# Four half-step curves in place of five whole-step curves for the exp on VectorE

## The chip, the cores and the metric

One core of one Trainium2 chip. Times are device microseconds (us) of one execution. "PE" in a profile is TensorE's matmuls, "PEld" its weight loads, "DVE" VectorE, "ACT" ScalarE, "POOL" GpSimd, "SP" SyncE.

## The reference

```python
x  = A_x                                # 1 x 2048 x 512, bf16
xn = layernorm(x)
q  = (xn @ wq)  as 32 heads of 16       # one key and one value head for all of them
k, v = xn @ wk, xn @ wv                 # 2048 x 16 each
p  = softmax(q k^T * 16**-0.5)          # 32 x 2048 x 2048 values of exp
s  = (p v) @ wo
g  = silu(silu(xn @ w1) @ w2)           # w1 512 x 1792, w2 1792 x 512
return x + s * g
```

The 32 x 2048 x 2048 = 134 million exps are what costs. In tiles of 128 keys x 512 queries they are 2048 "slots", in 32 groups of 64 (a group is four heads, one block of 512 queries and 16 blocks of 128 keys).

## The kernel before

Each slot's scores come from TensorE into a PSUM bank, go through exp, and the result is multiplied with v on TensorE. Two engines share the exps:

- ScalarE takes two or three slots in one exp instruction (128 x 1024 or 128 x 1536).
- VectorE is given no exp instruction. It writes the *bit pattern* of an approximate power of two: score x 128/ln 2 + offset, rounded to an integer and read as bf16. That is exact at powers of two and up to 6% too large between them. So five such curves, shifted by fifths of an octave, are weighted and added: the first is the pattern itself, the others are the pattern plus 25, 51, 77 and 102. The weights sit in five copies of v, so TensorE does the adding, with one product per curve.

```python
SHIFT = (0, 25, 51, 77, 102)
SHIFT_W = (0.2265625, 0.19726562, 0.17480469, 0.14941406, 0.12988281)
SHIFT_BETA = -0.239948630
K = len(SHIFT)
```

The instruction order is not written out by hand. A planner in the kernel, run when the kernel is built, simulates the engines with fixed durations and puts each next instruction where it fits. It is greedy: any small change can shift what it chooses later. It makes scores in turns called phases, each with two or three banks for ScalarE and up to two slots for VectorE. It decides slot by slot who computes an exp:

```python
        def want_d(banks_left=True):
            if st["assigned"] < 8:
                return False
            if any(k not in evac_kt or evac_kt[k].op is None for k in range(NKT)):
                return False
            if dve_backlog() > DVE_LIMIT:
                return False
            return True

...
                        cap = len([b for b in pool_free if pl.ready(PE, (), [("ps", b)]) <= t + 30])
                        bl = dve_backlog()
                        want = 2 if bl < TWO_LIMIT else 1
                        nd = min(cap, 4 - len(banks), len(need), want)
                        if nd < min(want, len(need)) and len(banks) == 3 and bl < LEND_LIMIT:
                            nd, lend = nd + 1, True
                        for i in need[:nd]:
```

So VectorE gets a slot when one of two spare PSUM banks is free (`pool_free`; the MLP's jobs borrow them too), or when a bank is lent from ScalarE's three, and its queue is short. ScalarE takes the other slots of the phase:

```python
                op = pl.place(AC, 0.8333 * NQ * n + T_AF, lambda a: a.activation(
                    pa_sb[:, s, 0:n * NQ], ps[:, b0 * 512:(b0 + n) * 512], ACT.Exp),
                    [("ps", b) for b in u.banks[:n]], [("pA", s)])
```

VectorE's part: one operation out of PSUM per slot (the pattern goes to `db_sb`, and its product is queued at once), and, for each batch of four slots, K - 1 = 4 shifts into `ds_sb`. A shift is one VectorE operation on 128 x 2048, or four GpSimd operations on 128 x 512, whichever engine gets to it first:

```python
                    tot[g, i] += K

                    def placed(pop, b=b, g=g, i=i, kt=kt, bt=bt):
                        if b in POOL_BANKS:
                            pool_free.append(b)
                        pvq[g][i].append((pop, v_lhs(0 + 1, g, kt), db_sb[:, bt.b, i * NQ:(i + 1) * NQ].bitcast(BF16),
                                          [("Db", bt.b, i)] + v_reads(1, kt), ("b", bt)))
                    bt.P[i] = pl.add(Task(DV, T_P, lambda v, b=b, i=i, bb=bt.b: v.tensor_scalar(
                        db_sb[:, bb, i * NQ:(i + 1) * NQ], bank(b), 128.0 * LOG2E, 128.0 * SHIFT_BETA + 16256.0,
                        op0=ALU.mult, op1=ALU.add), [("ps", b)], [("Db", bt.b, i)], 2 if b in POOL_BANKS else 0, on_place=placed))
...
            sh.whole = pl.add(Task(DV, T_SH, lambda v: v.tensor_scalar(
                ds_sb[:, s, :], db_sb[:, bt.b, :], SHIFT[j], None, op0=ALU.add),
                [("Db", bt.b, i) for i in range(4)], ds_keys(s),
                lambda: URGENT if bt.g == st["gO"] and nleft[bt.g] <= CLOSING else 6,
                list(bt.P.values()), on_place=placed_dv, ports=2))
            sh.chunks = []
            for i in range(4):
                tk = Task(PO, T_PC, lambda g, i=i: g.tensor_scalar(
                    ds_sb[:, s, i * NQ:(i + 1) * NQ], db_sb[:, bt.b, i * NQ:(i + 1) * NQ], 1.0, SHIFT[j],
                    op0=ALU.mult, op1=ALU.add),
                    [("Db", bt.b, i)], [("Ds", s, i)], (0 if i else 1, -len(shifts), i), list(bt.P.values()),
                    on_place=lambda pop, i=i: placed_po(pop, i),
                    gate=lambda i=i: (sh.owner is None if i == 0 else sh.owner == PO and sh.chunks[i - 1].op is not None)
                    and beside_psum_read(), ports=2)
...
        def beside_psum_read():
            if not pl.order[DV]:
                return False
            last = pl.order[DV][-1]
            return last.ports == 1 and last.end - max(pl.clk[PO], pl.lock[DV], pl.lock[PO]) >= PC_FIT * T_PC
```

The last function lets GpSimd start, in the plan, only beside a VectorE instruction that reads PSUM.

The softmax here doesn't subtract the row's maximum and nothing guards it: scores larger than these inputs give would overflow.

## Time and profile before

| | before |
|---|---|
| time, median of 3 runs | 750.44 us (750.18 to 750.54) |
| profiled span | 748.0 us |
| ScalarE busy | 727.6 us, 97% |
| TensorE busy | 709.1 us, 95% |
| VectorE busy | 703.7 us, 94% |
| GpSimd busy | 498.1 us, 67% |
| slots on ScalarE / VectorE | 1508 / 540 |
| exp instructions | 701 |

The page of the kernel before: its span, the busy time of each engine (us, share, instructions), and the chain of work that ended last, by engine and by line.

```profile
span 748.0 us, 21011 instructions
...
PE 709.1 (95%) x8809; PEld 200.9 (27%) x8809; DVE 703.7 (94%) x1226; ACT 727.6 (97%) x780; POOL 498.1 (67%) x686
...
ACT 95%; DVE 1%; PE 1%; DMA 1%; POOL 0%; issue 0%; SPq 0%; ACTq 0%; DVEq 0%
ACT pa_sb L1272 91%; ACT t_sb L539 4%; ACT t_sb L562 1%; DMA ds_sb<-in_A_x_dram 1%; DVE stats_sb L373 0%; PE ps L412 0%; POOL v_sb L496 0%; SPq L331 0%; PE ps L428 0%; DVE xn_sb L389 0%; PE ps L1034 0%; PE ps L711 0%; ACTq L277 0%; DVE ob_sb L579 0%; POOL rstd_sb L385 0%
```

Three engines are over 90% busy, so busy shares alone do not say which one sets the time. The chain does: followed back from the end, 95% of the span is ScalarE and 91% one line, the exp of score slots.

The table by stretches of the kernel before: stretch and length, then busy us and (instructions) of each engine, TensorE's granted clock, DMA share, GB/s.

```profile
core 0: us, PE busy (x) PEld busy (x) DVE busy (x) ACT busy (x) POOL busy (x), PEclk, DMA share, GB/s
0.00:25.00 25.00, 21.20 (x215) 10.23 (x219) 21.14 (x63) 14.07 (x16) 14.56 (x33) 0.93 0.90 296
...
300.00:400.00 100.00, 96.62 (x1212) 26.42 (x1204) 93.79 (x158) 100.00 (x107) 68.28 (x91) 1.00 0.01 2
...
700.00:735.00 35.00, 33.98 (x420) 9.13 (x420) 33.28 (x58) 35.00 (x39) 22.61 (x31) 1.00 0.01 2
```

After the start-up ScalarE is busy all of the time; VectorE and TensorE have 3 to 6% left.

Two pieces of the chain in order of time (start, length, what):

```profile
46.80 5.01 ACT pa_sb L1272 x5
...
99.11 4.58 ACT pa_sb L1272 x5
```

The second is five two-slot exps; the first, longer by just one slot, has one three-slot exp among four two-slot ones. So a two-slot exp takes 4.58 / 5 = 0.916 us from start to start and the three-slot one 5.01 - 4 x 0.916 = 1.346 us. The difference, 0.43 us, is the price of a slot on ScalarE; 0.916 - 2 x 0.43 = about 0.06 us is the fixed part of an instruction.

The groups of instructions of the kernel before: line, engine, operation, output<-input, shapes, count | busy us, mean ns of one | idle us of the engine just before, and what ended it.

```profile
L1272 ACT ACTIVATE pa_sb<-ps 128x1024 bf16<-128x1024 f32 x595 | 603.2, 1272 | 1.4 <-PE ps L711 1.3
L954 POOL TENSOR_SCALAR ds_sb<-db_sb 128x512 uint16<-128x512 uint16 x640 | 478.2, 758 | 215.1 <-DVE ds_sb L947 101.1 <-DVE db_sb L887 77.0 <-DVE otr_sb L1055 10.8
L887 DVE TENSOR_SCALAR db_sb<-ps 128x512 uint16<-128x512 f32 x540 | 357.2, 682 | 23.3 <-PE ps L711 21.2
L1034 PE MATMUL ps<-ds_sb,v_sb 128*32 128x512 bf16 x2160 | 286.7, 382 | 0.2
L711 PE MATMUL ps<-qt_sb,kt_sb 32*128 32x512 bf16 x2048 | 275.2, 384 | 28.4 <-ACT pa_sb L1272 14.7 <-DVE kt_sb L468 1.0 <-DVE f_sb L1051 1.0
...
L947 DVE TENSOR_SCALAR ds_sb<-db_sb 128x2048 uint16<-128x2048 uint16 x380 | 249.6, 682 | 1.5
L1272 ACT ACTIVATE pa_sb<-ps 128x1536 bf16<-128x1536 f32 x106 | 177.7, 1676 | 1.4 <-PE ps L711 1.4
L1034 PE MATMUL ps<-db_sb,v_sb 128*32 128x512 bf16 x540 | 145.0, 384 | 1.6 <-DVE f_sb L1051 1.6
```

595 x 2 + 106 x 3 = 1508 slots on ScalarE, and 540 on VectorE: 135 batches with 540 shifts, of which VectorE does 380 and GpSimd 160 (640 chunks / 4). The "mean ns" of an exp, 1272, is longer than its 0.916 us from start to start: successive instructions overlap, so a mean duration is no price. ScalarE's idle time before its exps is 2.8 us in all.

The waits of the kernel before: who waited for whom, us in total, times, longest.

```profile
PEld ps L711 <- ACT pa_sb L1272: 238.8, 514, 1.0
POOL ds_sb L954 <- DVE ds_sb L947: 101.1, 81, 3.5
```

TensorE's weight loads wait for ScalarE 238.8 us (a score bank is free only when exp has read it), ScalarE hardly ever for TensorE. GpSimd waits 101.1 us for VectorE's shifts. The Trainium skill ("SBUF — State Buffer", section "Who interferes with whom") says that VectorE in its two-port modes and GpSimd hold a shared port pair one at a time; this wait, put there by the planner's rule above, is how the plan keeps them apart. On the chip it does so only in part, and the trace agrees with the page: 384 of the 640 chunks meet no VectorE shift (less than 30 ns of it) and take 621 ns on average; the other 256 do and take 963 ns, and over all chunks the duration rises with the time shared (correlation 0.99). Of all 640 the least, median and greatest are 611, 618 and 1122 ns. So the mean of 758 ns is a mixture of the two kinds. (GpSimd's records are rough, so the sizes are too.)

### The profile page before, as it was taken

The numbers are of one execution on the slowest core, as the hardware profiler recorded it, in microseconds if no ns is written. First come the engines' busy times: TensorE is split into PE (matmuls) and PEld (weight loads), VectorE is DVE, ScalarE is ACT, GpSimd is POOL, SyncE is SP. The second block draws the span as 40 slices with busy tenths as digits, with TensorE's granted clock in tenths as the row PEclk, the third lists the DMA queues.
The fourth block names the chain that finished last, engine by engine and source line by source line (L and its number), as shares of the span: only waits on it lengthen the run. The fifth ranks groups of instructions, "written<-read, shape, count | busy, mean of one in ns | idle before, by whom it ended". The sixth has DMA issues, their size and how long they took to land.

```text
span 748.0 us, 21011 instructions
## 1 busy us (share of the span) xinstructions
PE 709.1 (95%) x8809; PEld 200.9 (27%) x8809; DVE 703.7 (94%) x1226; ACT 727.6 (97%) x780; POOL 498.1 (67%) x686
## 2 busy tenths in 40 slices
PE   8899999999999999999999999999999999999996
PEld 4322222222222222222222222222222222222222
DVE  8699999999999999998998999999999999999995
ACT  5899999999999999999999999999999999999994
POOL 5468674567767846766686766677678586676770
PEclk9999999999999999999999999999999999999999
DMA  9300000000000000000000000000000000000000
GB/s 314 95 4 2 2 1 2 2 2 3 2 1 16 11 21 16 1 3 2 2 2 3 15 20 26 2 2 2 1 2 2 16 16 15 16 2 2 2 2 29
DMA packets 11437, 12.65 MB, mean 17 GB/s; under 512 B 1808, under 2 KB 10768, under 8 KB 11344
## 3 DMA queue, kind: packets, MB, share of 16 engines
q1 hardware_dynamic: 10288, 11.28, 4.7%
q8 instruction: 71, 1.16, 0.6%
q10 hardware_dynamic: 1056, 0.03, 0.1%
q14 instruction: 22, 0.18, 0.1%
HBM read 8.95 MB, written 2.10 MB: 15 GB/s over the span
## 4 chain that ended last, share of the span: by engine, by line
ACT 95%; DVE 1%; PE 1%; DMA 1%; POOL 0%; issue 0%; SPq 0%; ACTq 0%; DVEq 0%
ACT pa_sb L1272 91%; ACT t_sb L539 4%; ACT t_sb L562 1%; DMA ds_sb<-in_A_x_dram 1%; DVE stats_sb L373 0%; PE ps L412 0%; POOL v_sb L496 0%; SPq L331 0%; PE ps L428 0%; DVE xn_sb L389 0%; PE ps L1034 0%; PE ps L711 0%; ACTq L277 0%; DVE ob_sb L579 0%; POOL rstd_sb L385 0%
## 5 line engine op out<-in xcount | busy, mean ns | idle before, releaser
L1272 ACT ACTIVATE pa_sb<-ps 128x1024 bf16<-128x1024 f32 (+1 forms) x701 | 715.5, 1333 | 2.8 <-PE ps L711 2.7
L954 POOL TENSOR_SCALAR ds_sb<-db_sb 128x512 uint16<-128x512 uint16 x640 | 478.2, 758 | 215.1 <-DVE ds_sb L947 101.1
L887 DVE TENSOR_SCALAR db_sb<-ps 128x512 uint16<-128x512 f32 x540 | 357.2, 682 | 23.3 <-PE ps L711 21.2
L711 PE MATMUL ps<-qt_sb,kt_sb 32*128 32x512 bf16 x2048 | 275.2, 384 | 28.4 <-ACT pa_sb L1272 14.7
L1034 PE MATMUL ps<-ds_sb,v_sb 128*32 128x512 bf16 x2160 | 286.7, 382 | 0.2
L1034 PE MATMUL ps<-pa_sb,v_sb 128*32 128x512 bf16 x1508 | 267.2, 385 | 1.1 <-ACT pa_sb L1272 0.7
L947 DVE TENSOR_SCALAR ds_sb<-db_sb 128x2048 uint16<-128x2048 uint16 x380 | 249.6, 682 | 1.5
L711 PEld LDWEIGHTS ps<-qt_sb,kt_sb 32*128 32x128 bf16 x2048 | 72.3, 91 | 332.6 <-ACT pa_sb L1272 238.8
L1034 PE MATMUL ps<-db_sb,v_sb 128*32 128x512 bf16 x540 | 145.0, 384 | 1.6 <-DVE f_sb L1051 1.6
L1034 PEld LDWEIGHTS ps<-ds_sb,v_sb 128*32 128x32 bf16 x2160 | 71.8, 95 | 54.7 <-issue 32.4
L412 PE MATMUL ps<-w_sb,u_sb 128*32 128x512 bf16 x896 | 79.0, 385 | 0.0
L412 PE MATMUL ps<-xnT_sb,w_sb 128*32 128x512 bf16 x896 | 76.3, 384 | 0.5 <-DVE u_sb L541 0.3
L1034 PEld LDWEIGHTS ps<-pa_sb,v_sb 128*32 128x32 bf16 x1508 | 64.1, 95 | 46.0 <-issue 31.7
L539 ACT ACTIVATE t_sb<-ps 128x512 bf16<-128x512 f32 x56 | 48.1, 858 | 0.0
L1034 PEld LDWEIGHTS ps<-db_sb,v_sb 128*32 128x32 bf16 x540 | 35.2, 94 | 17.3 <-issue 8.6
L541 DVE SCALAR_TENSOR_TENSOR u_sb<-t_sb,ps 128x512 bf16<-128x512 bf16 x56 | 38.0, 678 | 1.8 <-ACT t_sb L539 1.8
L412 PEld LDWEIGHTS ps<-xnT_sb,w_sb 128*32 128x32 bf16 x896 | 19.5, 94 | 31.7 <-issue 22.7
L412 PEld LDWEIGHTS ps<-w_sb,u_sb 128*32 128x32 bf16 x896 | 19.8, 94 | 30.5 <-issue 27.6
L1051 DVE STREAM_TRANSPOSE f_sb<-ps 128x512 f32<-128x512 f32 x32 | 22.6, 706 | 5.4 <-PE ps L1034 5.4
L412 PE MATMUL ps<-xnT_sb,wq_sb 128*32 128x512 bf16 x256 | 22.0, 384 | 0.2 <-DVE db_sb L887 0.2
L412 PE MATMUL ps<-wo_sb,on_sb 128*32 128x512 bf16 x256 | 20.0, 383 | 0.0
L496 POOL TENSOR_SCALAR v_sb<-v_sb 128x64 bf16<-128x64 f32 x24 | 8.9, 373 | 9.4 <-DVE v_sb L492 6.1
(47 smaller groups left out, 174.1 us busy)
## 6 DMA issues: line engine op xcount, KB each, us to landing
w_sb<-in_B_w_dram SPq DMA_DIRECT2D x2, 1792.0 KB, 13.6
xr_sb<-in_A_x_dram SPq DMA_DIRECT2D x16, 128.0 KB, 2.3
out_dram<-ob_sb SPq DMA_DIRECT2D x16, 128.0 KB, 1.7
ds_sb<-in_A_x_dram SPq DMA_DIRECT2D x3, 512.0 KB, 6.9
ds_sb<-in_A_x_dram SPq DMA_DIRECT2D x4, 128.0 KB, 2.6
wq_sb<-in_A_wq_dram SPq DMA_DIRECT2D x1, 512.0 KB, 5.0
wo_sb<-in_A_wo_dram SPq DMA_DIRECT2D x1, 512.0 KB, 15.3
kt_sb<-kt_sb SPq DMA_DIRECT2D x4, 64.0 KB, 2.3
```

The costliest lines, as they stand in the source:

```text
L412: last = h.matmul(bank(b)[32 * j:32 * (j + 1), 0:n], lhsT=lhs(j), rhs=rhs, start=start, stop=stop, tile_position=(0, 32 * j), skip_group_c ...
L496: v_task[c, j] = pl.add(Task(PO, 150.0, lambda g, j=j: g.tensor_scalar(v_sb[:, j, 4 * c:4 * c + 4, DH:2 * DH], v32_sb[:, 4 * c:4 * c + 4, ...
L539: t1 = Task(AC, 477.0, lambda a: a.activation(t_sb[:, k, :], bank(b), ACT.Tanh, scale=0.5), [("ps", b)], [("t", k)], 0)
L541: t2 = Task(DV, T_P, lambda v: v.scalar_tensor_tensor(out=u_sb[:, ft, :], in0=t_sb[:, k, :], scalar=1.0, in1=bank(b), op0=ALU.add, op1=ALU ...
L562: t1 = Task(AC, 477.0, lambda a: a.activation(t_sb[:, k, :], bank(b), ACT.Tanh, scale=0.25), [("ps", b)], [("t", k)], 0)
L711: return pe.matmul(bank(b), lhsT=kt_sb[32 * i:32 * i + 32, g % 2, kt * P:(kt + 1) * P], rhs=qt_sb[32 * i:32 * i + 32, (g // 2) % NQR, :], ...
L887: bt.P[i] = pl.add(Task(DV, T_P, lambda v, b=b, i=i, bb=bt.b: v.tensor_scalar(db_sb[:, bb, i * NQ:(i + 1) * NQ], bank(b), 128.0 * LOG2E, 1 ...
L947: sh.whole = pl.add(Task(DV, T_SH, lambda v: v.tensor_scalar(ds_sb[:, s, :], db_sb[:, bt.b, :], SHIFT[j], None, op0=ALU.add), [("Db", bt.b ...
L954: tk = Task(PO, T_PC, lambda g, i=i: g.tensor_scalar(ds_sb[:, s, i * NQ:(i + 1) * NQ], db_sb[:, bt.b, i * NQ:(i + 1) * NQ], 1.0, SHIFT[j], ...
L1034: h = pe.matmul(bank(OB)[32 * i:32 * (i + 1), :], lhsT=lhs, rhs=rhs, start=s0, stop=s1, tile_position=(0, 32 * i), skip_group_check=True)
L1051: t1 = pl.add(Task(DV, T_TR, lambda v: v.transpose(f_sb[:, k, :], bank(OB)), [("ps", OB)], [("F", k)], 1, [norm.get(("m", g - 2))]))
L1272: op = pl.place(AC, 0.8333 * NQ * n + T_AF, lambda a: a.activation(pa_sb[:, s, 0:n * NQ], ps[:, b0 * 512:(b0 + n) * 512], ACT.Exp), [("ps" ...
```

## The change

Its intent: four curves with the accuracy of five, and so four products per VectorE slot on TensorE, not five. VectorE keeps the pattern with one more bit of fraction (256 steps per octave). It is no longer a bf16 number, so it is never multiplied itself; each of the four shifts adds its amount and halves, and the rounding of the half goes down in two of the curves and up in the other two. The first product of a slot must now wait for a shift. A last clause lets GpSimd finish shifts at the end of the plan, when no PSUM read is left to work beside.

```diff
-SHIFT = (0, 25, 51, 77, 102)
-SHIFT_W = (0.2265625, 0.19726562, 0.17480469, 0.14941406, 0.12988281)
-SHIFT_BETA = -0.239948630
+SHIFT = (-0.5, 64.5, 127.5, 192.5)
+SHIFT_W = (0.24609375, 0.20703125, 0.173828125, 0.146484375)
+SHIFT_BETA = -0.035
...
-    NDB, NDS = 4, 2 * (K - 1)
+    NDB, NDS = 4, 2 * K
...
-            ... bt.left = g, {}, free[0], {}, 0, 4 + K - 1
+            ... bt.left = g, {}, free[0], {}, 0, K
...
-                        pvq[g][i].append((pop, v_lhs(0 + 1, g, kt), db_sb[...].bitcast(BF16), ...))
...
-                        db_sb[...], bank(b), 128.0 * LOG2E, 128.0 * SHIFT_BETA + 16256.0,
+                        db_sb[...], bank(b), 256.0 * LOG2E, 256.0 * (SHIFT_BETA + 127.0),
...
-                ds_sb[:, s, :], db_sb[:, bt.b, :], SHIFT[j], None, op0=ALU.add),
+                ds_sb[:, s, :], db_sb[:, bt.b, :], SHIFT[j - 1], 0.5, op0=ALU.add, op1=ALU.mult),
...
-                    ds_sb[...], db_sb[...], 1.0, SHIFT[j],
-                    op0=ALU.mult, op1=ALU.add),
+                    ds_sb[...], db_sb[...], SHIFT[j - 1], 0.5,
+                    op0=ALU.add, op1=ALU.mult),
...
+            if not any(... and tk.ports == 1 for tk in pl.tasks[DV]) and last.end <= pl.clk[PO]
+                    and st["assigned"] == NG * SLOTS:
+                return True
```

(The release of the pattern buffer and the index of the copies of v follow suit.)

Note what does not change: a batch still has four shifts.

More of the change, by code (lines that the diff above doesn't have):

```diff
@@ L746, in d_batch @@
             bt = Job()
-            bt.g, bt.slots, bt.b, bt.P, bt.nsh, bt.left = g, {}, free[0], {}, 0, 4 + K - 1
+            bt.g, bt.slots, bt.b, bt.P, bt.nsh, bt.left = g, {}, free[0], {}, 0, K
             return bt
@@ L884, in placed @@
                             pool_free.append(b)
-                        pvq[g][i].append((pop, v_lhs(0 + 1, g, kt), db_sb[:, bt.b, i * NQ:(i + 1) * NQ].bitcast(BF16),
-                                          [("Db", bt.b, i)] + v_reads(1, kt), ("b", bt)))
                     bt.P[i] = pl.add(Task(DV, T_P, lambda v, b=b, i=i, bb=bt.b: v.tensor_scalar(
-                        db_sb[:, bb, i * NQ:(i + 1) * NQ], bank(b), 128.0 * LOG2E, 128.0 * SHIFT_BETA + 16256.0,
+                        db_sb[:, bb, i * NQ:(i + 1) * NQ], bank(b), 256.0 * LOG2E, 256.0 * (SHIFT_BETA + 127.0),
                         op0=ALU.mult, op1=ALU.add), [("ps", b)], [("Db", bt.b, i)], 2 if b in POOL_BANKS else 0, on_place=placed))
@@ L905, in make_shifts @@
                     continue
-                while bt.nsh < K - 1:
+                while bt.nsh < K:
                     free = [k for k in range(NDS) if ds_busy[k] == 0 and (k < XB or x_free[0])]
@@ L927, in queue @@
                 kt = bt.slots[i]
-                pvq[bt.g][i].append((pop, v_lhs(j + 1, bt.g, kt), ds_sb[:, s, i * NQ:(i + 1) * NQ].bitcast(BF16),
-                                     [("Ds", s, i)] + v_reads(j + 1, kt), ("s", s)))
+                pvq[bt.g][i].append((pop, v_lhs(j, bt.g, kt), ds_sb[:, s, i * NQ:(i + 1) * NQ].bitcast(BF16),
+                                     [("Ds", s, i)] + v_reads(j, kt), ("s", s)))
             def placed_dv(pop):
@@ L954, in split @@
                 tk = Task(PO, T_PC, lambda g, i=i: g.tensor_scalar(
-                    ds_sb[:, s, i * NQ:(i + 1) * NQ], db_sb[:, bt.b, i * NQ:(i + 1) * NQ], 1.0, SHIFT[j],
-                    op0=ALU.mult, op1=ALU.add),
+                    ds_sb[:, s, i * NQ:(i + 1) * NQ], db_sb[:, bt.b, i * NQ:(i + 1) * NQ], SHIFT[j - 1], 0.5,
+                    op0=ALU.add, op1=ALU.mult),
                     [("Db", bt.b, i)], [("Ds", s, i)], (0 if i else 1, -len(shifts), i), list(bt.P.values()),
@@ L968, in beside_psum_read @@
             last = pl.order[DV][-1]
+            if not any(pl.avail(tk) is not None and not tk.after and tk.ports == 1 for tk in pl.tasks[DV]) and last.end <= pl.clk[PO] and st["assigned"] == NG * SLOTS:
+                return True
             return last.ports == 1 and last.end - max(pl.clk[PO], pl.lock[DV], pl.lock[PO]) >= PC_FIT * T_PC
@@ L1025, in do_pv @@
                         pa_busy[rel[1].slot] = 0
-                elif rel[0] == "b":
-                    release(rel[1])
                 else:
```

## The prediction

> **What bounds the kernel now.** ScalarE. The chain that ended last is ScalarE for 95% of the span, 91% of it the exp of score slots. ScalarE is busy 727.6 of 748.0 us, and 100% from 25 to 735 us in the table by stretches; it waits 2.8 us in all before its 701 exps (groups of instructions). In the chain five exps of two slots take 4.58 us, and five of which one has three slots take 5.01 us: a slot costs about 0.43 us, an instruction about 0.06 us more (estimates from these). VectorE (703.7 us, 94%) and TensorE (709.1 us, 95%) are close behind.
>
> The 2048 slots are split: 1508 to ScalarE (595 exps of two, 106 of three), 540 to VectorE. The planner inside the kernel gives VectorE a slot when a PSUM bank is free and its backlog is small. So time moves only if the split, or the number of exp instructions, moves.
>
> **What the change removes, adds and moves.**
> - TensorE: each VectorE slot has four weighted products, not five. The group "ps<-db_sb,v_sb" (540 matmuls) goes; four run side by side and such rounds start about 0.21 us apart in the timeline, so 135 x 0.21 = about 29 us of TensorE.
> - VectorE: still one operation of 512 from PSUM per slot (682 ns) and four shifts of 2048 per batch (682 ns). The shift has two operations in place of one. The Trainium skill ("VectorE: DVE Perf Modes", section on Mode 4x_2P) says that half of the ALU slices then hold the first operation and half the second, so the second is free; it gives 693 ns for 2048 elements, the trace has 682. I expect 682 again.
> - GpSimd: its chunk has two operations before and after: 758 ns.
> - Latency: a slot's first product now waits for a shift. The source buffer comes free sooner; counted in the planner of the kernel before, one was never lacking, so that is worth nothing.
>
> **How much is on the critical path.** None of the 29 us directly: ScalarE hardly waits for TensorE. Indirectly, jobs that borrow the two spare PSUM banks finish sooner, so a bank is free more often when scores are made (in the planner of the kernel before none was free in 122 of about 350 two-bank phases): more slots per phase, fewer exp instructions, more VectorE slots. But a VectorE slot costs VectorE about 0.68 + 0.7 x 0.68 = 1.1 us (380 of 540 shifts run there), and it idles only about 30 us between 25 and 735 us. It cannot take more than some 20 slots; I expect 10: 10 x 0.43 + 15 fewer instructions x 0.06 = about 5 us.
>
> **Prediction: 745 us**, range 736 to 752. Faster by over 2%: 7%. Within 2%: 91%. Slower by over 2%: 2%.
>
> **What would show each step.** The db_sb products gone, ds_sb products about 2200, TensorE down about 25 us to 91 to 93%. Shift groups still about 682 and 758 ns. VectorE slots 540 to 565, exps 670 to 700. ScalarE still 95% of the chain and 97% busy. VectorE 95 or 96%.
>
> **What would make it wrong.** If TensorE's load held the spare banks far more than I think, or GpSimd takes more of the shifts, VectorE slots could rise by 40 or more (725 to 735 us). If the planner's greedy order falls badly, 10 slots fewer and 755 us. If the two-operation shift lost its mode (over 1 us instead of 682 ns), VectorE would become the bound: tens of us more. If later first products leave exp buffers full, ScalarE would wait on TensorE.

## The result

The changed kernel takes 747.29 us (median of 4 runs, 747.09 to 747.95), against 750.49 us before (4 runs). The ratio is 0.9959, with a 95% interval of 0.9942 to 0.9977. The output is correct.

| | before | after |
|---|---|---|
| time, us | 750.49 | 747.29 |
| ScalarE busy, us | 727.6 | 725.6 |
| TensorE busy, us | 709.1 | 692.1 |
| VectorE busy, us | 703.7 | 705.8 |
| slots on ScalarE / VectorE | 1508 / 540 | 1504 / 544 |
| exp instructions | 701 | 696 |

The same lines of the changed kernel. Its page:

```profile
span 745.5 us, 19966 instructions
...
PE 692.1 (93%) x8289; PEld 195.0 (26%) x8289; DVE 705.8 (95%) x1232; ACT 725.6 (97%) x775; POOL 507.2 (68%) x689
...
ACT 95%; DVE 2%; PE 1%; DMA 1%; issue 0%; SPq 0%; DVEq 0%
ACT pa_sb L1270 91%; ACT t_sb L539 4%; ACT t_sb L562 1%; DMA ds_sb<-in_A_x_dram 1%; DVE stats_sb L373 1%; PE ps L711 0%; SPq L331 0%; PE ps L454 0%; PE ps L412 0%; PE ps L1032 0%; PE ps L428 0%; DVE xnT_sb L439 0%; DVE f_sb L1049 0%; DVE on_sb L1060 0%; DVE ob_sb L579 0%
```

Still ScalarE for 95% of the chain. Its table by stretches, with the columns as before:

```profile
300.00:400.00 100.00, 93.34 (x1125) 25.54 (x1123) 97.20 (x165) 100.00 (x107) 70.94 (x94) 1.00 0.01 2
...
700.00:735.00 35.00, 29.46 (x334) 8.47 (x333) 31.70 (x55) 35.00 (x35) 23.87 (x30) 1.00 0.01 2
```

TensorE has some more room and ScalarE none; VectorE is busy 671.8 of the 700 us from 25 to 725, against 668.3 before. Its groups:

```profile
L1270 ACT ACTIVATE pa_sb<-ps 128x1024 bf16<-128x1024 f32 x582 | 589.7, 1277 | 0.5 <-PE ps L711 0.5
L952 POOL TENSOR_SCALAR ds_sb<-db_sb 128x512 uint16<-128x512 uint16 x648 | 489.5, 766 | 207.4 <-DVE ds_sb L945 100.2 <-DVE db_sb L885 66.6 <-DVE otr_sb L1053 9.1
L885 DVE TENSOR_SCALAR db_sb<-ps 128x512 uint16<-128x512 f32 x544 | 358.8, 683 | 19.6 <-PE ps L711 17.7
L1032 PE MATMUL ps<-ds_sb,v_sb 128*32 128x512 bf16 x2176 | 292.2, 383 | 1.8 <-DVE f_sb L1049 0.5 <-DVE ds_sb L945 0.4 <-POOL ds_sb L952 0.3
L711 PE MATMUL ps<-qt_sb,kt_sb 32*128 32x512 bf16 x2048 | 274.0, 385 | 40.3 <-ACT pa_sb L1270 28.5 <-DVE qt_sb L519 1.0 <-DVE db_sb L885 0.5
...
L945 DVE TENSOR_SCALAR ds_sb<-db_sb 128x2048 uint16<-128x2048 uint16 x382 | 251.1, 682 | 1.4
L1270 ACT ACTIVATE pa_sb<-ps 128x1536 bf16<-128x1536 f32 x113 | 189.8, 1680 | 1.4 <-PE ps L711 1.4
```

The 540 products of `db_sb` are gone. The shift with two operations takes 682 ns, as the one with one did; GpSimd's chunk 766 ns (758 before), with a median of 617 (618 before). VectorE has one batch more (544 slots). ScalarE has four slots and five instructions fewer. Its waits:

```profile
PEld ps L711 <- ACT pa_sb L1270: 249.9, 529, 1.0
POOL ds_sb L952 <- DVE ds_sb L945: 100.2, 77, 3.2
```

TensorE's relief shows as longer waits for ScalarE: 249.9 us for weight loads (238.8 before) and 40.3 us of idle matmul time before scores (28.4). It was freed, and waits for the same engine as before.

TensorE lost 17 us, not the 29 us of the prediction. The products are issued in rounds of up to four, side by side. 2160 + 540 + 1508 = 4208 products need at least 1052 rounds, and 2176 + 1504 = 3680 need 920. Counted in the two plans, the kernel before uses 1088 rounds (1011 of them full) and the changed one 1005 (800 full): more of its rounds go out before four products are ready. 83 rounds fewer x 0.21 us (the distance of two rounds in the timeline of the kernel before) = 17 us. Nothing in the time depends on this, since ScalarE does not wait.

### The profile page after: what moved, and what is told of

It reads as the page before. It is cut to its first block, busy times and chain, and to the rows that moved or that the text cites. A ratio compares the mean times of both kernels' runs of the same rounds, so it can differ in the third digit from the quotient of the medians. Undisturbed runs are those within 1.5% of the kernel's fastest.

```text
span 745.5 us, 19966 instructions
## 1 busy us (share of the span) xinstructions
PE 692.1 (93%) x8289; PEld 195.0 (26%) x8289; DVE 705.8 (95%) x1232; ACT 725.6 (97%) x775; POOL 507.2 (68%) x689
## 4 chain that ended last, share of the span: by engine, by line
ACT 95%; DVE 2%; PE 1%; DMA 1%; issue 0%; SPq 0%; DVEq 0%
ACT pa_sb L1270 91%; ACT t_sb L539 4%; ACT t_sb L562 1%; DMA ds_sb<-in_A_x_dram 1%; DVE stats_sb L373 1%; PE ps L711 0%; SPq L331 0%; PE ps L454 0%; PE ps L412 0%; PE ps L1032 0%; PE ps L428 0%; DVE xnT_sb L439 0%; DVE f_sb L1049 0%; DVE on_sb L1060 0%; DVE ob_sb L579 0%
## 5 line engine op out<-in xcount | busy, mean ns | idle before, releaser
L952 POOL TENSOR_SCALAR ds_sb<-db_sb 128x512 uint16<-128x512 uint16 x648 | 489.5, 766 | 207.4 <-DVE ds_sb L945 100.2
L711 PE MATMUL ps<-qt_sb,kt_sb 32*128 32x512 bf16 x2048 | 274.0, 385 | 40.3 <-ACT pa_sb L1270 28.5
L1032 PE MATMUL ps<-ds_sb,v_sb 128*32 128x512 bf16 x2176 | 292.2, 383 | 1.8 <-DVE f_sb L1049 0.5
L1032 PE MATMUL ps<-pa_sb,v_sb 128*32 128x512 bf16 x1504 | 260.9, 385 | 2.7 <-DVE f_sb L1049 1.6
L711 PEld LDWEIGHTS ps<-qt_sb,kt_sb 32*128 32x128 bf16 x2048 | 71.7, 91 | 333.7 <-ACT pa_sb L1270 249.9
L412 PE MATMUL ps<-w_sb,u_sb 128*32 128x512 bf16 x896 | 80.9, 386 | 0.0
L412 PE MATMUL ps<-xnT_sb,w_sb 128*32 128x512 bf16 x896 | 78.1, 385 | 0.5 <-DVE u_sb L541 0.4
L539 ACT ACTIVATE t_sb<-ps 128x512 bf16<-128x512 f32 x56 | 47.0, 840 | 0.0
L562 ACT ACTIVATE t_sb<-ps 128x512 bf16<-128x512 f32 x16 | 13.6, 848 | 0.0
L1053 DVE TENSOR_TENSOR otr_sb<-f_sb,rcp_sb 128x256 bf16<-128x256 f32 x32 | 13.3, 415 | 0.1
```

The lines of the kernel that those rows point to most:

```text
L412: last = h.matmul(bank(b)[32 * j:32 * (j + 1), 0:n], lhsT=lhs(j), rhs=rhs, start=start, stop=stop, tile_position=(0, 32 * j), skip_group_c ...
L539: t1 = Task(AC, 477.0, lambda a: a.activation(t_sb[:, k, :], bank(b), ACT.Tanh, scale=0.5), [("ps", b)], [("t", k)], 0)
L562: t1 = Task(AC, 477.0, lambda a: a.activation(t_sb[:, k, :], bank(b), ACT.Tanh, scale=0.25), [("ps", b)], [("t", k)], 0)
L711: return pe.matmul(bank(b), lhsT=kt_sb[32 * i:32 * i + 32, g % 2, kt * P:(kt + 1) * P], rhs=qt_sb[32 * i:32 * i + 32, (g // 2) % NQR, :], ...
L952: tk = Task(PO, T_PC, lambda g, i=i: g.tensor_scalar(ds_sb[:, s, i * NQ:(i + 1) * NQ], db_sb[:, bt.b, i * NQ:(i + 1) * NQ], SHIFT[j - 1], 0.5,
L1032: h = pe.matmul(bank(OB)[32 * i:32 * (i + 1), :], lhsT=lhs, rhs=rhs, start=s0, stop=s1, tile_position=(0, 32 * i), skip_group_check=True)
```

## Experiments

**Theory 1**: ScalarE sets the time, by the number of its slots and instructions. How many slots it gets is capped, at given thresholds of the planner, by VectorE's and GpSimd's shift work, which the change leaves as it was. TensorE's relief only moves the planner's choices a little. From the numbers above, the time should be 750.0 - 0.43 x (VectorE slots - 540) + 0.06 x (exps - 701).

**Rivals:** (2) TensorE's load sets the split, so less of it is worth time; (3) the two-operation shift or the late first product costs something that hid a larger gain; (4) the 3 us are the luck of a greedy planner.

All runs below had five rounds against the kernel before, whose own median was 749.76, 750.53 and 750.00 us in the three sets (runs 1 to 4, 5 to 8, 9 and 10; each set on another chip). "Planned" counts were read from the built program before the run. Two of the kernels leave a curve out and so have wrong exps on VectorE; the comparison with the reference is blind to the quality of the exp here.

### 1. The relief without the new form

```diff
 (kernel before)
-                        pvq[g][i].append((pop, v_lhs(0 + 1, g, kt), db_sb[...], ..., ("b", bt)))
-            bt.left = 4 + K - 1;   tot[g, i] += K
+            bt.left = K - 1;       tot[g, i] += K - 1
+            (the clause for the end of the plan, as in the change)
```

> The kernel before with its first, unshifted product left out: four products per VectorE slot, all four from one-operation shifts, the old bit pattern; values of the VectorE slots are wrong on purpose (one of five curves is missing). Its planned order has the same 544 VectorE slots and 696 exps as the changed kernel. Theory 1 (only the TensorE relief and what the planner makes of it matter): 747.3 us, within 1.5 us of the changed kernel. Rival (the two-operation shift or the half-bit pattern costs time that hid a larger gain): 3 us or more below the changed kernel, with a shift group clearly shorter than 682 ns or a GpSimd chunk below 758 ns.

Measured: 747.59 us (746.79 to 748.55), ratio 0.9973 (0.9960 to 0.9985); VectorE's shift group 680 ns, GpSimd's chunk 770 ns (median 621). Within 0.3 us of the changed kernel. The half-step pattern and the second operation cost nothing visible; that part of rival 3 is out.

### 2. Five products put back

```diff
 (changed kernel)
-SHIFT_W = (0.24609375, ...
+SHIFT_W = (0.123046875, ...
-                pvq[bt.g][i].append((pop, v_lhs(j, ...
+                for _ in range(2 if j == 1 else 1):
+                    pvq[bt.g][i].append((pop, v_lhs(j, ...
+            (and the counters of products and of buffer uses to match)
```

> The changed kernel with the first curve's product issued twice at half its weight: right result, 29 us of TensorE put back, VectorE, GpSimd and the late first product as in the changed kernel. Planned: 536 VectorE slots, 702 exps. Theory 1: ScalarE gets 8 slots and 6 exps more, 8 x 0.43 + 6 x 0.06 = 3.8 us longer than the changed kernel, so 751 us (749.5 to 752.5). Rival (the gain is luck of the planner's order, not TensorE): 747 to 749 us.

Measured: 752.13 us (750.47 to 752.60), ratio 1.0037 (1.0023 to 1.0051); TensorE busy 711.7 us, ScalarE 729.3 us with 702 exps, 536 VectorE slots. From its page:

```profile
PE 711.7 (95%) x8793; PEld 200.8 (27%) x8793; DVE 701.4 (94%) x1222; ACT 729.3 (97%) x781; POOL 492.9 (66%) x665
```

With TensorE's load back ScalarE gets eight slots more, and the time follows. By itself this cannot say whether the eight slots are TensorE's doing or the planner's draw; runs 6 and 7 and the counts below them bear on that.

### 3. Three products

```diff
 (changed kernel; def queue(pop, i) of the shifts)
+                if j == K:
+                    ds_busy[s] -= 1
+                    return
                 pvq[bt.g][i].append(...)
-                    tot[g, i] += K
+                    tot[g, i] += K - 1
```

> The changed kernel with the fourth curve still computed but never multiplied: three products per slot, wrong values on purpose. TensorE loses 29 us more, the work of VectorE and GpSimd per slot is unchanged. Planned: the same 544 VectorE slots, 685 exps. Theory 1 (TensorE is not the currency; VectorE slots are capped by VectorE): TensorE busy under 675 us, time 746.5 us (745 to 748). Rival (time follows TensorE's load): another 3 us or more, 744 us or below.

Measured: 746.86 us (746.18 to 748.68), ratio 0.9969 (0.9955 to 0.9983). From its page:

```profile
PE 669.8 (90%) x7917; PEld 190.1 (26%) x7917; DVE 705.4 (95%) x1232; ACT 725.2 (97%) x764; POOL 514.6 (69%) x689
...
L1273 ACT ACTIVATE pa_sb<-ps 128x1024 bf16<-128x1024 f32 (+1 forms) x685 | 712.8, 1352 | 0.8 <-PE ps L711 0.6
...
L948 DVE TENSOR_SCALAR ds_sb<-db_sb 128x2048 uint16<-128x2048 uint16 x382 | 252.1, 680 | 1.5
```

Another 22 us off TensorE, 692.1 to 669.8, and the time stays with the changed kernel's. VectorE still has 544 slots and 382 shifts of its own. Rival 2 is out for this step: the 22 us buy nothing clear of the scatter.

### 4. Four curves with three shifts

```diff
 (kernel before)
-SHIFT = (0, 25, 51, 77, 102)
-SHIFT_W = (0.2265625, 0.19726562, 0.17480469, 0.14941406, 0.12988281)
-SHIFT_BETA = -0.239948630
+SHIFT = (0, 32, 64, 96)
+SHIFT_W = (0.283203125, 0.23828125, 0.2001953125, 0.1689453125)
+SHIFT_BETA = -0.238722873
-    NDB, NDS = 4, 2 * (K - 1)
+    NDB, NDS = 4, 8
+            (the clause for the end of the plan, as in the change)
```

> The kernel before with four curves in its own form: the pattern used as it is, and three shifts (32, 64, 96) with weights refitted; right result but for a slightly coarser exp. TensorE has four products as in the changed kernel, but VectorE and GpSimd have three shifts per batch, not four. Planned: 592 VectorE slots, 704 exps. Theory 1 (VectorE's time per slot sets the split): 48 slots fewer on ScalarE than in the changed kernel, 48 x 0.43 = 21 us, so about 728 us (724 to 734), ScalarE still over 95% busy. Rival (TensorE's relief is what counts, and it is the same here): 745 to 748 us.

Measured: 728.93 us (728.88 to 729.35), ratio 0.9726 (0.9713 to 0.9740), in the range. Its page:

```profile
PE 690.1 (95%) x8429; PEld 189.9 (26%) x8429; DVE 675.1 (93%) x1176; ACT 705.7 (97%) x783; POOL 502.9 (69%) x705
...
L1274 ACT ACTIVATE pa_sb<-ps 128x1024 bf16<-128x1024 f32 (+1 forms) x704 | 690.8, 1280 | 3.1 <-PE ps L711 3.0
L954 POOL TENSOR_SCALAR ds_sb<-db_sb 128x512 uint16<-128x512 uint16 x664 | 485.2, 747 | 194.7 <-DVE db_sb L887 107.6
L887 DVE TENSOR_SCALAR db_sb<-ps 128x512 uint16<-128x512 f32 x592 | 388.3, 681 | 19.7 <-PE ps L711 17.7
...
L947 DVE TENSOR_SCALAR ds_sb<-db_sb 128x2048 uint16<-128x2048 uint16 x278 | 186.2, 681 | 1.7
```

VectorE takes 592 slots; a batch has three shifts, 278 on VectorE and 166 (664 / 4) on GpSimd. It is *less* busy than in the changed kernel (675.1 us) because the whole kernel is shorter. TensorE has as many products per slot as the changed kernel, and is 95% busy. So the same relief of TensorE that gave 3 us there gives 21 us here, when a shift is dropped with it.

### 5. The dropped shift put back as a dummy

```diff
 (kernel of run 4; def queue(pop, i) of the shifts)
-SHIFT = (0, 32, 64, 96)
+SHIFT = (0, 32, 64, 96, 112)
-                    tot[g, i] += K
+                    tot[g, i] += K - 1
+                if j == K - 1:
+                    ds_busy[s] -= 1
+                    return
                 pvq[bt.g][i].append(...)
```

> direct_plus_three with a fourth shift computed and never multiplied: right result, the shift work of VectorE and GpSimd back at four per batch, TensorE at four products, the first product early as in the kernel before. Planned: 544 VectorE slots, 694 exps. Theory 1 (the shift work per batch sets the split): the whole gain of direct_plus_three goes, 747 us (745.5 to 748.5). Rival (the gain of direct_plus_three came from the early first product or its constants): 735 us or below. It also shows whether the late first product of the changed kernel costs anything: if so, this is 2 us or more below 747.3.

Measured: 748.17 us (746.60 to 749.33), ratio 0.9965 (0.9951 to 0.9979). Its page:

```profile
L1277 ACT ACTIVATE pa_sb<-ps 128x1024 bf16<-128x1024 f32 (+2 forms) x694 | 712.2, 1329 | 2.6 <-PE ps L711 2.4
...
L887 DVE TENSOR_SCALAR db_sb<-ps 128x512 uint16<-128x512 f32 x544 | 357.4, 680 | 18.9 <-PE ps L711 17.1
...
L950 DVE TENSOR_SCALAR ds_sb<-db_sb 128x2048 uint16<-128x2048 uint16 x383 | 252.1, 682 | 1.2
```

A shift that is computed and never used takes back the whole gain: 592 slots become 544. VectorE's group does 383 shifts again, not 278. That settles that the shift, and not TensorE's relief, the new constants or the number of buffers (eight in runs 4 and 5), moved the split by 48 slots; runs 8 to 10 show that the planner's thresholds move it too. Its first product is early, as in the kernel before, and it is no faster than the changed kernel, so the late first product costs nothing visible either: rival 3 is out in both parts.

### 6 and 7. One planner constant moved

```diff
 (6: kernel before)                      (7: changed kernel)
-MARGIN, MARGIN_END = 16, 28            -S_TOL = 30.0
+MARGIN, MARGIN_END = 14, 28            +S_TOL = 25.0
```

> The kernel before with one planner constant moved (MARGIN 16 to 14), nothing else: five products, TensorE as loaded as before. Planned: 544 VectorE slots, 705 exps. Theory 1 (time follows the count on ScalarE, and such counts scatter with any small change of the planner): 4 slots fewer and 4 exps more than before, 748.5 us (747.5 to 749.5), half of the change's gain with no relief of TensorE. Rival (the gain is TensorE's relief alone): no change, 750 us.

> The changed kernel with one planner constant moved (S_TOL 30 to 25). Planned: 540 VectorE slots, 695 exps. Theory 1: 4 slots more on ScalarE than in the changed kernel, 749 us (748 to 750), so that about half of its gain goes while TensorE keeps its whole relief. Rival (relief of TensorE is the gain): 747.3 us.

Measured: 749.49 us (747.23 to 749.94), ratio 0.9980 (0.9967 to 0.9993) for run 6; 749.00 us (747.18 to 751.60), ratio 0.9988 (0.9970 to 1.0006) for run 7. Both lie where the counts put them: a constant that has nothing to do with the change moves the kernel before half the way to the changed one, and the changed one half the way back. Run 7 by itself is inconclusive, since its interval includes 1, and its runs scatter by 4 us.

To see how much of the gain is the draw, the planner of the kernel before (with the clause for the end), of the changed kernel and of run 2 were each run with 21 settings of seven of its constants near their values, and the instructions of the built programs counted; none of these was run on the chip but those told here.

| 21 settings | VectorE slots, mean (range) | exps, mean (range) |
|---|---|---|
| kernel before | 540.6 (536 to 544) | 702.2 (699 to 705) |
| changed kernel | 542.3 (540 to 544) | 694.8 (692 to 699) |
| five products (run 2) | 540.0 (536 to 548) | 702.5 (699 to 706) |

So TensorE's relief is worth on average 1.7 x 0.43 + 7.4 x 0.06 = about 1.2 us (an estimate from the two prices). That is less than the step of one batch, 4 x 0.43 = 1.7 us, by which the draw scatters. Of its two parts only the fall in exps is clear, since the ranges of the slots overlap. 21 other settings (MARGIN, TWO_LIMIT, LEND_LIMIT, S_TOL, HOLD, PRESS and DVE_LIMIT, one moved at a time) were built: the kernel before with the clause and the changed kernel both had 541.5 slots on average, and the exps fell from 703.9 to 695.0, worth about 0.5 us. So TensorE's relief is worth some 0.5 to 1.2 us by these counts, which no run on the chip separates from the draw. At the constants of the two kernels as timed the counts differ by 2.0 us; what goes beyond the relief is the draw (rival 4). The last 1.2 us of the measured 3.2 no count explains. They may be scatter: the interval of the ratio, 1.7 to 4.4 us, includes 2.0.

The count shows one more thing: without the clause for the end, the planner of the kernel before stops with work left over in 9 of the 21 settings; with it, in none. At the constants as they were, the clause alone leaves the counts of all engines as they were.

### 8. The three-shift kernel with its thresholds moved

```diff
 (kernel of run 4)
-LEND_LIMIT = 3000.0
-TWO_LIMIT = 1500.0
+LEND_LIMIT = 3500.0
+TWO_LIMIT = 2250.0
-NPA, PRESS = 9, 4
+NPA, PRESS = 9, 5
```

> direct_plus_three with three thresholds of the planner moved (TWO_LIMIT 1500 to 2250, LEND_LIMIT 3000 to 3500, PRESS 4 to 5), right result. Planned: 604 VectorE slots, 703 exps. Theory 1: 12 slots fewer on ScalarE, 5 us, so 724 us (720 to 726), ScalarE 97% busy. Rival (VectorE's share is already as large as it can be): 728 us or more, with ScalarE waiting for TensorE.

Measured: 722.46 us (721.88 to 724.05), ratio 0.9628 (0.9614 to 0.9643). Its page:

```profile
PE 687.0 (95%) x8461; PEld 188.9 (26%) x8461; DVE 679.4 (94%) x1188; ACT 700.5 (97%) x782; POOL 526.3 (73%) x741
...
L1274 ACT ACTIVATE pa_sb<-ps 128x1024 bf16<-128x1024 f32 (+1 forms) x703 | 686.9, 1275 | 2.4 <-PE ps L711 2.1
...
L887 DVE TENSOR_SCALAR db_sb<-ps 128x512 uint16<-128x512 f32 x604 | 396.3, 681 | 18.9 <-PE ps L711 16.2
```

604 slots on VectorE. This version beats both kernels, by 3.7% against the kernel before. Its price is in the exp. Worked out from the constants (the weighted sum of the curves over the true power, at 20,000 points of one octave, with rounding to the nearest whole step, which no run here tests), the relative deviation has a standard deviation of 0.17% in the kernel before, 0.14% in the changed kernel and 0.19% here. So by this reckoning the change buys accuracy, which the clock does not show; who can live with 0.19% gets 28 us.

### 9 and 10. The same threshold in both kernels

```diff
 (9: kernel before and the clause)       (10: changed kernel)
-TWO_LIMIT = 1500.0                     -TWO_LIMIT = 1500.0
+TWO_LIMIT = 2000.0                     +TWO_LIMIT = 2500.0
```

> The kernel before with one threshold moved (TWO_LIMIT 1500 to 2000: it may take two VectorE slots in a phase at a larger backlog) and the change's escape for the end of the plan, which alone leaves the order of instructions as it was. Planned: 552 VectorE slots, 704 exps. Theory 1: 12 slots fewer and 3 exps more on ScalarE, 750 - 5.2 + 0.2 = 745 us (744 to 746.5): more gained by a threshold than by the change. Rival (TensorE, still at five products, holds it): 749 us or more.

> The changed kernel with the same threshold moved (TWO_LIMIT 1500 to 2500), right result. Planned: 552 VectorE slots, 703 exps, the same as the kernel before with its threshold moved. Theory 1 (VectorE caps both forms at the same number): 744.5 us (743 to 746), level with before_two2000, so that the change gains nothing once both are set to their best. Rival (four products allow a better split): 742 us or below.

Measured: 744.55 us (743.76 to 746.37), ratio 0.9925 (0.9910 to 0.9940) for run 9; 746.41 us (743.80 to 747.35), ratio 0.9942 (0.9924 to 0.9960) for run 10, just outside its range. With a threshold moved, the kernel *before* gains 5 us with all five products, more than the change brought. And both kernels end at the same 552 slots. The slots came out of VectorE's idle time. The stretch from 25 to 725 us of the kernel before and of run 9, columns as before:

```profile
25.00:725.00 700.00, 672.45 (x8405) 185.71 (x8397) 668.30 (x1139) 700.00 (x752) 478.88 (x648) 1.00 0.02 7
25.00:725.00 700.00, 677.22 (x8449) 185.17 (x8451) 681.52 (x1168) 699.90 (x759) 504.91 (x674) 1.00 0.02 7
```

VectorE's idle time there falls from 31.7 to 18.5 us while ScalarE stays busy. TensorE is then close to a second bound: it has 5% of run 9's chain, against 1% in the kernel before and 2% in run 10. Run 10's miss is taken up below.

### The scatter within a kernel and TensorE's clock

Each run has its mean granted TensorE clock, and within a kernel the times follow it. Taking from every run the means of its kernel, 88 runs of 12 kernels give 0.415 us less per 0.001 of clock, with a correlation of -0.83. Where the clock is missing can be read from the table by stretches. Run 7's profiled execution (clock 0.999, 747.18 us), columns as before:

```profile
16.00:25.00 9.00, 7.83 (x108) 3.45 (x107) 8.56 (x26) 8.58 (x8) 4.75 (x11) 1.00 0.86 283
25.00:725.00 700.00, 658.18 (x7935) 180.19 (x7933) 672.52 (x1145) 700.00 (x748) 481.29 (x639) 1.00 0.02 7
725.00:746.00 21.00, 12.19 (x157) 4.46 (x157) 9.39 (x18) 10.89 (x11) 0.00 (x0) 0.96 0.08 26
```

and run 10's (clock 0.991, 746.37 us):

```profile
16.00:25.00 9.00, 8.82 (x92) 3.66 (x90) 7.08 (x21) 6.71 (x7) 3.72 (x9) 0.72 0.86 285
25.00:725.00 700.00, 662.48 (x7980) 177.96 (x7976) 681.29 (x1168) 699.22 (x759) 504.95 (x673) 1.00 0.02 7
725.00:746.00 21.00, 11.60 (x155) 4.37 (x152) 9.92 (x19) 10.07 (x10) 1.31 (x3) 0.89 0.07 26
```

From 25 us on to 725 us both have the full clock. Between 16 and 25 us one has 1.00 and the other 0.72, and in the last 21 us one 0.96 and the other 0.89. In the first of these stretches ScalarE does 8.58 us of work with the full clock and 6.71 with the lower one, so it falls behind there. This is a correlation with a place, in two kernels with different plans, and not an experiment: no run changed the start-up.

Set to the same clock, 0.997, with that slope, the kernels line up with the count of theory 1:

| kernel | slots / exps | mean us (clock) | at clock 0.997 | from the counts |
|---|---|---|---|---|
| before | 540 / 701 | 750.16 (0.9965) | 750.0 | 750.0 (set) |
| after | 544 / 696 | 747.40 (0.9962) | 747.1 | 748.0 |
| 1 relief, old form | 544 / 696 | 747.50 (0.9976) | 747.8 | 748.0 |
| 2 five products | 536 / 702 | 751.94 (0.9936) | 750.5 | 751.8 |
| 3 three products | 544 / 685 | 747.21 (0.9964) | 747.0 | 747.3 |
| 4 direct and three | 592 / 704 | 729.02 (0.9980) | 729.4 | 727.8 |
| 5 dummy shift | 544 / 694 | 747.98 (0.9947) | 747.0 | 747.9 |
| 6 before, MARGIN 14 | 544 / 705 | 749.09 (0.9955) | 748.5 | 748.5 |
| 7 after, S_TOL 25 | 540 / 695 | 749.27 (0.9967) | 749.1 | 749.6 |
| 8 direct and three, tuned | 604 / 703 | 722.71 (0.9965) | 722.5 | 722.6 |
| 9 before, TWO_LIMIT 2000 | 552 / 704 | 744.92 (0.9970) | 744.9 | 745.0 |
| 10 after, TWO_LIMIT 2500 | 552 / 703 | 745.91 (0.9927) | 744.1 | 745.0 |

Two prices read from two lines of the chain reproduce the other eleven kernels within 1.6 us over a range of 28 us. Setting the clock equal does not make the fit better: without it (counted from the 750.16 us of the kernel before) the counts miss by 0.4 us on average and 1.2 at most, with it by 0.6 and 1.6. So the slope describes the scatter within a kernel and is not shown to hold between kernels. Run 10's mean lies 0.9 us above its count before the setting and 0.9 below after it; that its low clock made it miss its range is likely but not shown.

## Why the prediction was right, point by point

- *ScalarE bounds the kernel; 29 us of TensorE are not on the critical path.* Right. Run 3 takes another 22 us from TensorE for nothing.
- *The second operation of a shift is free.* Right: 682 ns with one and with two. The Trainium skill's account ("VectorE: DVE Perf Modes", section "Mode 4×_2P"), with half of the slices for each operation, fits that number, though a trace does not show slices; run 1 has the changed kernel's time with the one-operation shift.
- *GpSimd's chunk unchanged.* Right: the medians are 618 ns before, 617 after, and 621 in run 1 with the old form. The means (758, 766, 770) differ by how many chunks meet a VectorE shift, not by the operations.
- *The late first product costs nothing.* Right (run 5).
- *TensorE down about 25 us.* Mis-sized: 17.0 us. The term "135 x 0.21" took the rounds as full; the plan has 83 rounds fewer, not 132, because it issues more partial ones.
- *A spare bank is free more often.* Wrong in the phases that the prediction counted, and hardly true in all. Counted in the two plans, over the phases in which VectorE could have taken a slot: two-bank phases with no spare bank rose from 122 to 141; three-bank phases with none fell from 250 to 215, so in all 372 became 356. The jobs do leave earlier (of all phases, about 700, those with no job on a spare bank rose from 26 to 92), so it must be VectorE's own waiting slots that hold the banks instead.
- *About 10 VectorE slots and 15 fewer instructions, 5 us.* Mis-sized: 4 slots and 5 instructions, 4 x 0.43 + 5 x 0.06 = 2.0 us of ScalarE (busy 727.6 and 725.6 us: just that), and 3.2 us of time. On average over planner settings 1.7 slots and 7.4 instructions. VectorE's 30 us of idle time were there to be filled, but relief of TensorE does not fill them; from 25 to 725 us the planner leaves 4.5% in the kernel before and 4.0% in the changed one, and a threshold fills 13 us of it (run 9).
- *747.29 us* lies in the range of 736 to 752 and is "within 2%". The bound, the free shift and the smallness of the gain were foreseen for the right reasons. That the number came within 2.3 us is partly luck: the range would have held with no change at all (750.49 us), the path that was to bring the gain (a spare bank free more often) is hardly there, and part of the 3.2 us is the draw. What the prediction lacked is that the planner's draw scatters by as much as the expected gain.

## What to carry to other kernels

When work is shared between two engines, find the price of a share on each (here 0.43 us per slot on ScalarE, and the shift work per batch on VectorE and GpSimd) and change the price; relief of a third engine, though it is 95% busy, mostly freed it to wait here. Before a curve, a term or a pass is removed, ask which of its costs goes: of five curves the one that was removed here was the only one that cost its engine no shift. And where a greedy planner lays out the kernel, count what it builds for a handful of neighbouring settings before a gain of half a per cent is put down to a cause; one threshold was worth more than the change.

## What the Trainium skill lacked or had wrong

- "ScalarE: Activation LUTs" (section "What ACT_TABLE_LOAD costs") gives an instruction as 186 ns + 0.833 ns per element (280 ns with one operand per partition), and an overlap of about 93 ns between successive ones: for 1024 elements 1039 or 1133 ns alone, and 946 or 1040 ns from start to start. Here, from PSUM, the mean duration is 1272 ns and start to start 916 ns (1346 ns for 1536 elements): durations longer, and an overlap of 1272 - 916 = 356 ns.
- "VectorE: DVE Perf Modes" agrees for the shift (693 ns given, 682 measured). Its conditions name 16-bit tensors, not what is done to them; that a uint16 stream with a fractional amount and a halving keeps the mode is not stated outright, and it does (682 ns).
- "GPSIMD Engine Reference" (section "Elementwise — side-by-side cycle accounting") gives 768 ns for 512 elements of a tight custom loop. The built-in two-operation form on uint16, not listed, had a median of 617 to 622 ns in the twelve kernels here; the averages of 745 to 777 ns include chunks that overlap a VectorE shift.
- "TensorE: Matmul & The Clock Gate" describes the clock's warm-up for TensorE alone. No page says what it does to a kernel bound by another engine: here runs of one kernel differ by up to 4.4 us, 0.415 us per 0.001 of mean granted clock, and in the two executions compared the clock was short only in the first 25 and the last 21 us.
- "Perfetto Trace Analysis" (section "Identifying the Most-Contended Engine") names the engine with the highest occupancy, but for TensorE it sets matmul busy time aside and takes MFU (the share of peak arithmetic) and the busy share of the weight loads. With ScalarE at 97%, VectorE at 94% and weight loads at 27% that pointed the right way here; the chain of waits and run 3 confirm it. Nothing to correct.
